# Experts' products on four 128x32 column parts, and routing steps placed by another estimate

## The chip, the cores and the metric

The kernel runs on one core of a Trainium2 chip. TensorE (PE) multiplies, VectorE (DVE), ScalarE (ACT) and GpSimd (POOL) compute, and SyncE (SP) issues most transfers. The metric is the device time of one launch in microseconds: the median of 3 runs is 492.07 (491.12 to 495.2).

## What is computed

```python
scores = scale * np.matmul(q, k.transpose(0, 1, 3, 2))      # batch 8, 12 heads, 448 tokens, 64 each
scores = cap * np.tanh(scores / cap)
attn = softmax(scores); x = (attn @ v) as 3584 tokens x 768
logits = x @ w_gate                                          # 8 experts
expert_idx = np.argmax(logits, axis=1); gate_w = its softmax weight
for e in range(E):
    tok_idx = tokens of expert e; if over 80, the 80 of largest gate_w are kept
    h = np.maximum(x[tok_idx] @ w1[e], 0.0)                  # 768 -> 1024
    out[tok_idx] = gate_w[tok_idx, None] * (h @ w2[e])       # 1024 -> 768, other rows zero
```

All is float32.

## The kernel before

Attention runs in 24 units: 8 batches, and in each three groups of four heads. A unit has seven tiles of scores (`scores`, L1152 and L1160) in two PSUM buffers, each followed by a tanh on ScalarE (L1161), then four exponentials (`expo`, L1165). GpSimd adds exponents for the divisor (`esum`, L1171). One unit later TensorE multiplies by the values (`av` L1192, `rests` L1223 and L1225), VectorE turns the divisor (`sums` L1233), scales (`scaled` L1245) and transposes (`turned` L1253). Units in DIRECT (20 and 23) take the divisor by products of ones instead (`total_of` L1210). The order in a unit is the string STEPS; unit 0 uses it too.

Behind every third unit a batch is routed: logits (L1270), their turn (`lt` L1285), the choice and key (L296 to L316), and the rank of every token's key among its expert's, by comparisons on VectorE that TensorE adds up (`ranks`, `late_ranks`: `psk`, `gb`, `pd`). Batches 0 to 4 are pruned first (`prt` L634, `prk` L649), so that experts 0 to 3 of the list can start early: their rows are gathered from DRAM by GpSimd (L783) and laid by VectorE (L678). Experts 4 and 5 have to wait for all batches (L756, L783, L1561). `background` places these steps between the steps of a unit: three lists (urgent, low, bg) of steps with a cost in ns, which it holds against clocks of TensorE and VectorE, by the tables PLACE and SLACK.

LAST is the order of the passage: the values of unit 23, and in between the six chunks of expert 0's first product (`begin`). Then come the products of six experts, 6 chunks of w1 (768x1024) and 8 of w2 (1024x768) each, as `chunk` writes them (L842): 96 token columns stationary, weights moving, F32. For expert 4 and 5's first product and expert 3 to 5's second, `wsplit` splits each weight chunk into two rounded halves on ScalarE (L830) and VectorE (L832), and three faster products take the place of one. SP loads the weights (L823) into 8 buffers that are filled during attention and 6 more. `turn` transposes the hidden rows (L870, L879), `put` scales by the gate (L899) and GpSimd stores the rows by an indirect transfer (L900).

## Time and profile before

| | us |
|---|---|
| median of 3 runs | 492.07 |
| profiled run | 495.86 |
| its span | 494.1 |
| TensorE busy | 459.2 (93%) |
| ScalarE busy | 338.6 (69%) |
| VectorE busy | 273.5 (55%) |
| GpSimd busy | 219.3 (44%) |
| TensorE's mean granted clock | 0.976 of 2.4 GHz |

The busy times are shares of the whole span; the stages of the program have different limits, so windows by stage are read beside them. Times in rows count from the start of the span.

### The profile page before, as it was taken

The numbers are of one execution on the slowest core, as the hardware profiler recorded it, in microseconds if no ns is written. First come the engines' busy times: TensorE is split into PE (matmuls) and PEld (weight loads), VectorE is DVE, ScalarE is ACT, GpSimd is POOL, SyncE is SP. The second block draws the span as 40 slices with busy tenths as digits, with TensorE's granted clock in tenths as the row PEclk, the third lists the DMA queues.
The fourth block names the chain that finished last, engine by engine and source line by source line (L and its number), as shares of the span: only waits on it lengthen the run. The fifth ranks groups of instructions, "written<-read, shape, count | busy, mean of one in ns | idle before, by whom it ended". The sixth has DMA issues, their size and how long they took to land. (4 is left out here: it accounts for less than half of the span.)

```text
span 494.1 us, 18314 instructions
## 1 busy us (share of the span) xinstructions
PE 459.2 (93%) x7945; PEld 232.1 (47%) x7945; DVE 273.5 (55%) x785; ACT 338.6 (69%) x360; POOL 219.3 (44%) x136
## 2 busy tenths in 40 slices
PE   7799999999999999999999989968999999975992
PEld 4244544544444544444454534532345445653781
DVE  1033374355456557645756928750658595657682
ACT  3999899899989889979888977950022101456681
POOL 0577656656656656666566315624150001440000
PEclk9999999999999999999999999997999999988897
DMA  6557687696596596676258576551099998999411
GB/s 161 146 170 197 192 238 222 185 257 190 168 257 192 158 290 192 190 194 167 87 126 218 141 213 168 162 190 36 8 342 391 400 359 263 334 398 356 123 62 27
DMA packets 67768, 100.89 MB, mean 204 GB/s; under 512 B 12208, under 2 KB 50128, under 8 KB 67680
## 3 DMA queue, kind: packets, MB, share of 16 engines
q1 hardware_dynamic: 66048, 96.23, 64.1%
q0 software_dynamic: 1440, 3.25, 2.0%
q8 instruction: 64, 1.05, 0.9%
q14 instruction: 24, 0.20, 0.1%
q10 hardware_dynamic: 192, 0.17, 0.1%
HBM read 76.11 MB, written 23.80 MB: 202 GB/s over the span
## 5 line engine op out<-in xcount | busy, mean ns | idle before, releaser
L1161 ACT ACTIVATE e<-sc 128x896 f32<-128x896 f32 x168 | 150.8, 913 | 35.7 <-PE sc L1160 24.7
L1192 PE MATMUL av<-e,vr 64*32 64x448 f32 x2304 | 161.1, 539 | 1.5 <-DVE x L1245 1.5
L1160 PE MATMUL sc<-qt,kt 64*32 64x448 f32 x2304 | 144.7, 545 | 4.9 <-ACT e L1161 3.4
L1165 ACT ACTIVATE e<-e 128x896 f32<-128x896 f32 (+1 forms) x96 | 144.7, 1507 | 0.8
L1171 POOL TENSOR_TENSOR t<-e 128x896 f32<-128x896 f32 x44 | 92.9, 2111 | 95.3 <-ACT e L1165 95.3
L1173 POOL TENSOR_TENSOR t<-t,e 128x896 f32<-128x896 f32 x44 | 92.9, 2112 | 36.5 <-ACT e L1165 34.8
L1192 PEld LDWEIGHTS av<-e,vr 64*32 64x32 f32 x2304 | 54.8, 107 | 58.1 <-issue 45.6
L1233 DVE STREAM_TRANSPOSE st<-sp 128x448 f32<-128x448 f32 x24 | 15.6, 650 | 118.4 <-PE sp L1192 96.5
L1160 PEld LDWEIGHTS sc<-qt,kt 64*32 64x32 f32 x2304 | 43.7, 107 | 52.0 <-issue 36.2
L842 PE MATMUL hp<-w,xt 128*96 128x512 f32 x96 | 45.5, 616 | 4.9 <-DVE xt L678 4.9
L1225 PE MATMUL av<-e,vr 64*32 64x224 f32 x384 | 44.3, 349 | 0.0
L1192 PE MATMUL sp<-t,ones 64*32 64x448 f32 x352 | 42.9, 536 | 0.0
L1225 PE MATMUL av<-e,vx 64*32 64x224 f32 x384 | 42.3, 350 | 0.0
L900 POOL DMA_INDIRECT out_dram<-ysv,si x6 | 6.1, 1016 | 81.0 <-ACT ysv L899 73.3
L1245 DVE TENSOR_TENSOR x<-av,r 128x448 f32<-128x448 f32 x48 | 27.7, 620 | 17.9 <-PE av L1192 17.8
L842 PE MATMUL yp<-w,thv 128*96 128x384 f32 x96 | 32.1, 487 | 0.0
L1225 PEld LDWEIGHTS av<-e,vr 64*32 64x32 f32 x384 | 22.0, 107 | 19.0 <-issue 18.6
L423 DVE TENSOR_SCALAR_CACHE_REDUCE gb<-krow,kc 112x896 bf16<-112x896 f32 (+7 forms) x36 | 30.1, 883 | 0.0
L1223 PE MATMUL sp<-e,ones 64*32 64x224 f32 x384 | 28.8, 350 | 0.0
L1253 DVE STREAM_TRANSPOSE xb<-x 128x448 f32<-128x448 f32 x48 | 27.9, 619 | 0.0
L1152 PE MATMUL sc<-qt,kt 64*32 64x224 f32 x768 | 25.6, 361 | 2.2 <-DMA qt<-in_q_dram 1.4
L842 PEld LDWEIGHTS hp<-w,xt 128*96 128x96 f32 x96 | 15.2, 167 | 26.2 <-issue 20.5
(281 smaller groups left out, 549.5 us busy)
## 6 DMA issues: line engine op xcount, KB each, us to landing
w<-in_w_dram SPq DMA_DIRECT2D x36, 512.0 KB
w<-in_w_dram SPq DMA_DIRECT2D x48, 384.0 KB
vr<-in_v_dram SPq DMA_DIRECT2D x24, 512.0 KB
out_dram<-zero SPq DMA_DIRECT2D x14, 768.0 KB
xs<-xb SPq DMA_DIRECT2D x32, 336.0 KB
kt<-in_k_dram SPq DMA_DIRECT2D x46, 224.0 KB
qt<-in_q_dram SPq DMA_DIRECT2D x46, 224.0 KB
vx<-in_v_dram SPq DMA_DIRECT2D x48, 32.0 KB
```

The lines of the kernel that those rows point to most:

```text
L423: nc.vector.tensor_scalar(g, krow[:, x:y], kp, 0.0, op0=ALU.is_ge, op1=ALU.add, accum_out=a)
L842: nc.tensor.matmul(ps[nn][:, 0:m] if isinstance(ps, tuple) else ps[:, nn, 0:m], a[:, kk, :], bb[:, nn * m:(nn + 1) * m], start=(kk == 0 an ...
L1160: nc.tensor.matmul(ps[32 * m:32 * m + 32, h, :S], st["k", u][w, pr, y:y + 32], st["q", u][w, pr], start=True, stop=True)
L1161: nc.scalar.activation(st["e", u][:, 2 * x:2 * x + 2], ps[:, :, :S], AF.Tanh, scale=st["regs"][0])
L1165: nc.scalar.activation(e, e, AF.Exp, scale=st["regs"][1])
L1171: nc.gpsimd.tensor_tensor(t1, e[:, 0:2], e[:, 2:4], op=ALU.add)
L1173: nc.gpsimd.tensor_tensor(st["es", u, pr], st["es", u, pr], e[:, 4:6], op=ALU.add)
L1192: behind(nc.tensor.matmul(ps[32 * g:32 * g + 32, :S], v_, e, start=first, stop=final))
L1223: behind(nc.tensor.matmul(st["sp", u][32 * g:32 * g + 32, HQ * i:HQ * i + HQ], ones[w, 0:32], e, start=(part == 0), stop=False))
L1225: behind(nc.tensor.matmul(st["av", u, f][32 * g:32 * g + 32, HQ * i:HQ * i + HQ], last_of(u, pr, h, i)[w, 32 * f:32 * f + 32], e, start=Fa ...
L1245: nc.vector.tensor_tensor(st["x", u][:, f], st["av", u, f][:, :S], st["r", u], op=ALU.mult)
L1253: nc.vector.transpose(st["xt", b][:, :, j, :], st["x", u][:, f].rearrange("p (a b) -> p a b", b=32))
```

## The change

Each chunk of an expert's weights is multiplied in four column parts: for a group of 32 tokens the same 128x32 stationary tile stands in four column strips, and each strip takes a quarter of the weight columns. The results lie on 128 partitions, so `relu`, `turn` and `put` work on 128 partitions, and a quarter row is stored per index: three indirect transfers of 128 quarter rows per expert instead of one of 96 rows. Gates are gathered three times for four experts together and copied. Nothing is split or rounded any more. Ten more weight buffers follow the first eight instead of six.

The scale of tanh and exp is a 128x1 pointer instead of a register. Unit 0 runs by FIRST, with the tile of the last keys (`q0`, `e3`) at its end. Unit 20 takes its divisor by `esum`. Two tiny VectorE steps get a summed output. `background` has a fourth list (fill), new costs, and steps that name what they need and what they finish.

```diff
-WMORE = 6
-AHEAD = 2
-DIRECT = (20, 23)
-WHOLE = (4, 3)
+WMORE = 10
+DIRECT = (23,)
...
-                nc.vector.tensor_scalar(usb, u, 2.0 ** -28, None, op0=ALU.max)
+                nc.vector.tensor_scalar(usb, u, 2.0 ** -28, 0.0, op0=ALU.max, op1=ALU.add, accum_out=dump[:C])
...
-                nc.gpsimd.indirect_dma_start(out=gt0[:, v:v + 1], out_offset=None, in_=gd[0:OB * S],
...
+    def gates_at(to, sg, g, n, m):
+        nc.gpsimd.indirect_dma_start(out=to[0:32 * n, g:g + 1], out_offset=None, in_=gd[0:m],
+                                     in_offset=bass.IndirectOffsetOnAxis(ap=sg[0:32 * n, g:g + 1], axis=0))
...
-    def wsplit(fp, w, n, tag):
-
-        hi = fp.tile([128, F], F32R, name=f"wh{tag}", tag="wh", bufs=AHEAD + 1)
-        nc.scalar.copy(hi[:, :n], w)
-        lo = fp.tile([128, F], F32R, name=f"wl{tag}", tag="wl", bufs=AHEAD + 1)
-        nc.vector.tensor_tensor(lo[:, :n], w, hi[:, :n].bitcast(F32), op=ALU.subtract)
-        return hi, lo
+    def rows_of(x, kk):
+
+        return lambda g: x[:, kk, 32 * g:32 * g + 32]
+
+    def turned_rows(x, kk):
+
+        j, b = divmod(kk, 2)
+        return lambda g: x[:, 2 * g + b, 32 * j:32 * j + 32]
+
+    def spot(ps, g, n):
+
+        return ps[g // 2][:, QF * (g % 2):QF * (g % 2) + n] if isinstance(ps, tuple) else ps[:, g // 2, QF * (g % 2):QF * (g % 2) + n]
 
     def chunk(ps, x, w, kk, last, n):
 
-        m = n // 2
-        pairs = [(x[0], w[0]), (x[1], w[0]), (x[0], w[1])] if len(w) == 2 else [(x[-1], w[0])]
-        terms = [(nn, i) for i in range(len(pairs)) for nn in range(2)]
-        for nn, i in sorted(terms) if kk == last else terms:
-            a, bb = pairs[i]
-            nc.tensor.matmul(ps[nn][:, 0:m] if isinstance(ps, tuple) else ps[:, nn, 0:m], a[:, kk, :], bb[:, nn * m:(nn + 1) * m],
-                             start=(kk == 0 and i == 0), stop=(kk == last and i == len(pairs) - 1))
+        q = n // 4
+        of = (rows_of if n == F else turned_rows)(x, kk)
+        for g in range(NG):
+            for j in range(4):
+                nc.tensor.matmul(spot(ps, g, q)[32 * j:32 * j + 32], of(g), w[:, q * j:q * j + q],
+                                 start=(kk == 0 and g % 2 == 0), stop=(kk == last and g > 0))
...
+        for i in range(2 * NG):
+            nc.tensor.transpose(hv[:, i], hs[:, i], cst("ident"))
+        nc.scalar.copy(th, hv)
+        return th
...
-            nc.scalar.activation(ys, yp[:, :, 0:DM // 2], AF.Copy, scale=gt)
...
+            for g in range(NG):
+                nc.scalar.activation(ys[:, g], spot(yp, g, QD), AF.Copy, scale=gt[:, g:g + 1])
+        for g in range(NG):
+            w = nc.gpsimd.indirect_dma_start(out=out.rearrange("t (i c) -> (t i) c", c=QD), out_offset=bass.IndirectOffsetOnAxis(ap=si[:, g:g + 1], axis=0),
+                                             in_=ys[:, g], in_offset=None, bounds_check=4 * T - 1, oob_is_err=False)
...
-            nc.scalar.activation(st["e", u][:, 2 * x:2 * x + 2], ps[:, :, :S], AF.Tanh, scale=st["regs"][0])
+            nc.scalar.activation(st["e", u][:, 2 * x:2 * x + 2], ps[:, :, :S], AF.Tanh, scale=scl)
...
-            nc.scalar.activation(e, e, AF.Exp, scale=st["regs"][1])
+            nc.scalar.activation(e, e, AF.Exp, scale=capt)
...
-            for q, last in ((urgent, 1), (low, 3), (bg, 2)):
+            for q, last in ((urgent, 1), (low, 3), (bg, 2), (fill, 4)):
...
-                        if now[0] < now[last] + gap or (n in (0, 1) and clock[0] < max(st["read"], ready_at[last] if gap else 0)):
+                        need = getattr(f, "needs", None)
+                        if need is not None:
+                            if clock[0] < max(st["read"], done.get(need, 1e18)):
+                                break
+                        elif now[0] < now[last] + gap or (n in (0, 1) and clock[0] < max(st["read"], ready_at[last] if gap else 0)):
                             break
...
-        st["regs"] = [nc.scalar.alloc_register(n) for n in ("sclr", "capr")]
-        for reg, t in zip(st["regs"], (scl, capt)):
-            nc.scalar.reg_load(reg, t[0:1, 0:1].bitcast(I32))
...
+        FIRST = "q1 q2 q3 e0 q4 p00 q5 e1 p01 l q6 e2 p10 p11 q0 e3".split()
...
-            todo = STEPS if w < NU else LAST
+            todo = FIRST if w == 0 else STEPS if w < NU else LAST
```

How the order moves, at three places.

TensorE's first tiles, unit 0 (`sc0_n`: tile n of unit 0; tile 0 holds the last keys of all four heads, tiles 1 to 3 belong to the first pair). Before, and now:

```order
L1152 MATMUL sc0_0_212<-qt0_156,kt0_157 32x224 x16
L1160 MATMUL sc0_1_230<-qt0_156,kt0_157 32x448 x8
L1160 MATMUL sc0_2_241<-qt0_156,kt0_157 32x448 x8
L1160 MATMUL sc0_3_251<-qt0_156,kt0_157 32x448 x8
...
L1160 MATMUL sc0_6_291<-qt0_156,kt0_157 32x448 x8
L1152 MATMUL sc1_0_312<-qt1_205,kt1_206 32x224 x16
```

```order
L1205 MATMUL sc0_1_211<-qt0_155,kt0_156 32x448 x8
L1205 MATMUL sc0_2_221<-qt0_155,kt0_156 32x448 x8
L1205 MATMUL sc0_3_231<-qt0_155,kt0_156 32x448 x8
L1205 MATMUL sc0_4_242<-qt0_155,kt0_156 32x448 x8
...
L1197 MATMUL sc0_0_285<-qt0_155,kt0_156 32x224 x16
L1197 MATMUL sc1_0_311<-qt1_204,kt1_205 32x224 x16
```

Tile 0 went from the first place to the last of its unit.

TensorE around the passage: the multiplication that gathers the places (`prt`, 20 products of which the first stands here), the key transposes (`prk`) and expert 0's first product (`hp0`). Before, and now:

```order
L1160 MATMUL sc23_4_5495<-qt23_5175,kt23_5176 32x448 x8
...
L634 MATMUL prt_5522<-prrh_5397,prlh_5172 96x40
...
L1160 MATMUL sc23_5_5543<-qt23_5175,kt23_5176 32x448 x8
...
L1160 MATMUL sc23_6_5595<-qt23_5175,kt23_5176 32x448 x8
...
L649 MATMUL prk0_5671<-ctt_74,prx_5586 112x96 x4
L649 MATMUL prk1_5677<-ctt_74,prx_5586 112x96 x4
L842 MATMUL hp0_5693<-w0_0_4869,xt0_0_109 96x512 x2
...
L842 MATMUL hp0_5693<-w0_1_4871,xt0_0_109 96x512 x2
```

```order
L1205 MATMUL sc22_4_5323<-qt22_4977,kt22_4978 32x448 x8
...
L652 MATMUL prt_5352<-prrh_5193,prlh_5032 96x40
...
L1205 MATMUL sc22_5_5380<-qt22_4977,kt22_4978 32x448 x8
...
L1205 MATMUL sc23_4_5589<-qt23_5198,kt23_5199 32x448 x8
...
L667 MATMUL prk0_5616<-ctt_74,prx_5462 112x96 x4
L1205 MATMUL sc23_5_5622<-qt23_5198,kt23_5199 32x448 x8
...
L667 MATMUL prk1_5663<-ctt_74,prx_5462 112x96 x4
L1205 MATMUL sc23_6_5669<-qt23_5198,kt23_5199 32x448 x8
...
L891 MATMUL hp0_5756<-w0_0_4911,xt0_0_110 32x256 x12
...
L891 MATMUL hp0_5756<-w0_1_4913,xt0_0_110 32x256 x12
```

`prt` moved from unit 23 to unit 22, `prk` from behind unit 23's scores to between them, and a chunk is twelve products of 32x256 instead of two of 96x512.

VectorE at the same stretch: the table of places (`prtk`, `tks`), the row numbers for the gathers (`gi0`), expert 0's rows (`xt0_0`), the sums of units 22 and 23 (`st22`, `st23`) and batch 5's gates (`w25`, `grow`). Before, and now:

```order
L1233 STREAM_TRANSPOSE st22_5562<-sp22_5448 128x448
...
L654 TENSOR_TENSOR prtk_5590<-tab_96 96x4
L656 COPY tks_104<-prtk_5590 32x4 x3
...
L662 TENSOR_SCALAR gi0_105<-prga_5627 32x12 x4
...
L678 STREAM_TRANSPOSE xt0_0_109<-xge0_0_5683 128x6x32
L678 STREAM_TRANSPOSE xt0_0_109<-xge0_1_5685 128x6x32
L678 STREAM_TRANSPOSE xt0_0_109<-xge0_2_5687 128x6x32
L1233 STREAM_TRANSPOSE st23_5752<-sp23_5662 128x448
```

```order
L672 TENSOR_TENSOR prtk_5466<-tab_96 96x4
L674 COPY tks_104<-prtk_5466 32x4 x3
...
L784 TENSOR_SCALAR gi0_105<-prga_5471 32x12 x4
...
L1278 STREAM_TRANSPOSE st22_5641<-sp22_5528 128x448
...
L691 STREAM_TRANSPOSE xt0_0_110<-xge0_0_5701 128x6x32
L691 STREAM_TRANSPOSE xt0_0_110<-xge0_1_5703 128x6x32
L691 STREAM_TRANSPOSE xt0_0_110<-xge0_2_5705 128x6x32
...
L330 SCALAR_TENSOR_TENSOR w25_5806<-tau5_5038,rd5_5042 112x32
...
L339 STREAM_TRANSPOSE grow_80<-gcol_79 128x32
L1278 STREAM_TRANSPOSE st23_5867<-sp23_5744 128x448
```

The row numbers moved ahead of the sums of unit 22, and batch 5's gates ahead of those of unit 23.

## Rows read from the trace of the kernel before

**Rows 1.** the head of the page.

```profile
span 494.1 us, 18314 instructions
```

**Rows 2.** windows of the run: length; busy us of PE, PEld, DVE, ACT, POOL; PEclk, DMA share, GB/s.

```profile
9.71:327.94 318.23, 309.92 (x7138) 146.94 (x7124) 171.77 (x485) 284.98 (x282) 185.81 (x88) 1.00 0.69 190
327.94:357.60 29.66, 24.23 (x205) 8.77 (x204) 11.71 (x51) 1.42 (x5) 8.79 (x10) 0.88 0.15 46
357.60:484.64 127.04, 118.58 (x558) 71.98 (x556) 88.65 (x243) 50.02 (x69) 22.79 (x26) 0.96 0.82 295
...
382.85:395.20 12.35, 12.35 (x41) 5.44 (x40) 7.16 (x15) 2.25 (x3) 1.28 (x2) 1.00 1.02 399
```

**Rows 3.** what TensorE waited for: us in total, times, longest us.

```profile
PE hp L842 <- DVE xt L678: 4.9, 1, 4.9
PE hp5a L842 <- ACT xh L1562: 4.5, 1, 4.5
PE sc L1160 <- ACT e L1161: 3.4, 4, 1.4
...
PE psk L404 <- DVE kc L316: 1.9, 1, 1.9
PE sc L1160 <- issue: 1.5, 1, 1.5
PE av L1192 <- DVE x L1245: 1.5, 1, 1.5
```

**Rows 4.** TensorE in the experts' stage: start us, us, engine, line, operation, count.

```profile
354.12 7.03 PE L842 MATMUL hp<-w,xt 128*96 128x512 f32 x16
360.98 0.83 PE L870 MATMUL htv<-ctt,hsv 96*128 96x96 f32 x8
361.74 1.96 PE L842 MATMUL hp<-w,xt 128*96 128x512 f32 x4
363.62 1.34 PE L1270 MATMUL lgp<-x,wgt 128*32 128x224 f32 x24
```

**Rows 5.** routing on TensorE in the experts' stage by line: busy us, mean ns.

```profile
L512 PE MATMUL pd<-ones_b,gb 112*128 112x1 bf16 x45 | 1.7, 164 | 0.3 <-DVE gl L487 0.2
...
L1270 PE MATMUL lgp<-x,wgt 128*32 128x224 f32 x24 | 1.3, 357 | 0.0
...
L1270 PEld LDWEIGHTS lgp<-x,wgt 128*32 128x32 f32 x24 | 0.7, 109 | 1.0 <-issue 0.8
```

**Rows 6.** the logits' weight loads, columns as in rows 4.

```profile
363.62 0.92 PEld L1270 LDWEIGHTS lgp<-x,wgt 128*32 128x32 f32 x24 [0.79 <-issue]
```

**Rows 7.** ScalarE by line and shape: busy us, mean ns, idle before.

```profile
L899 ACT ACTIVATE ysv<-yp,gt 96x768 f32<-96x768 f32 x4 | 3.6, 897 | 18.2 <-PE yp L842 14.0 <-DMA out_dram<-ysv,si 2.4 <-issue 1.8
...
L872 ACT COPY thv<-htv 128x768 f32<-128x768 f32 x3 | 2.4, 799 | 11.5 <-PE htv L870 11.5
```

**Rows 8.** the start: TensorE, columns as in rows 4.

```profile
5.17 1.13 PE L1152 MATMUL sc<-qt,kt 64*32 64x224 f32 x16 [0.74 <-DMA kt<-in_k_dram]
```

**Rows 9.** the first tanh on ScalarE, columns as in rows 4.

```profile
9.71 0.92 ACT L1161 ACTIVATE e<-sc 128x896 f32<-128x896 f32 x1 [5.93 <-PE sc L1152]
```

**Rows 10.** VectorE in batch 5's routing, columns as in rows 4.

```profile
233.45 1.87 DVE L315 TENSOR_SCALAR us<-u 112x4 f32<-112x4 f32 x1
```

**Rows 11.** VectorE as attention ends: sums, places, rows of expert 0.

```profile
323.66 0.65 DVE L1233 STREAM_TRANSPOSE st<-sp 128x448 f32<-128x448 f32 x1 [2.67 <-PE sp L1192]
...
335.54 0.38 DVE L678 STREAM_TRANSPOSE xt<-xge 128x192 f32<-128x192 f32 x1 [0.83 <-DMA xge<-xs,gi]
```

**Rows 12.** TensorE as attention ends.

```profile
335.97 3.73 PE L842 MATMUL hp<-w,xt 128*96 128x512 f32 x4 [4.87 <-DVE xt L678]
```

**Rows 13.** GpSimd: first gather of late rows, and the last store.

```profile
425.71 1.00 POOL L783 DMA_INDIRECT xgv<-xs,gi  x1 [7.03 <-DVE sz L774]
...
485.81 0.92 POOL L900 DMA_INDIRECT out_dram<-ysv,si  x1 [7.43 <-ACT ysv L897]
```

**Rows 14.** VectorE: last part of expert 4's rows laid.

```profile
434.65 0.38 DVE L1561 STREAM_TRANSPOSE xt<-xgv 128x192 f32<-128x192 f32 x1 [1.07 <-DMA xgv<-xs,gi]
```

More of the change, by code (lines that the diff above doesn't have):

```diff
@@ L56 @@
 LATER = OB * NQ + 1
-SLACK = (5500, 4000, 2500, 1500, 1800, 8000)
+SLACK = (6700, 5200, 3700, 1800, 2000, 9350)
 LATE = 3
@@ L391, in final_order, with known, waits @@
         return f0, f1, f2, f6, f3, f4, f5, f8
+    def known(f, done=None, needs=None):
+        if done is not None:
+            f.done = done
+        if needs is not None:
+            f.needs = needs
+        return f
+    def waits(f, n=1):
+        f.waits = n
+        return f
     def ranks(krow, gp, pl, b, acc, dfc, x0, c0, blocks, gw=GW):
@@ L535, in late_ranks @@
                 yield rest(i)
-        yield 200, use(1, after), 1
-        yield 200, use(-1, add), 1
+        yield 20, use(1, after, 600), 1
+        yield 130, use(-1, add), 1
     def fold(eng, t, dst):
@@ L690, in prune @@
+        yield 450, known(heads, "heads"), 0
+        yield 20, known(use(0, counts, 500), needs="heads"), 1
         steps = order(sm)
         for i, f in enumerate(steps):
[L692 to L694 removed]
+            yield 600 if f is steps[-1] else 750 if i == 1 else 450, waits(f), int(i == 0)
@@ L695, in prune @@
+        yield 2050, waits(lambda: z.update(r=ranked(sm, OCOL, acc, dfc, higher(sm, neso, cst("gt", C).rearrange("p (a e) -> p a e", a=E), "o"))), 2), 0
+        yield 500, places, 0
         for i in range(2):
-            yield 900, lambda i=i: parts(i), 0
-        for i in range((OCOL + 7) // 8):
-            yield 1500, lambda i=i: left(i), 0
+            yield 700, waits(lambda i=i: parts(i)), 0
+        for i in range((OCOL + 3) // 4):
+            yield 500, waits(lambda i=i: left(i)), 0
@@ L707, in prune @@
+        yield 700, waits(early), 0
+        yield 900, waits(rows_in), 0
+        yield 1900, waits(rows_out), 0
         for h in range(2):
-            yield 200, use(0, lambda h=h: rows(h)), 1
+            yield 20, use(0, lambda h=h: rows(h), 700), 1
         yield 50, lambda: low.extend(first_rows()), 0
@@ new lines, in gate_rows, with gates_of @@
+    def gate_rows(a, sg, n):
+        for e in range(n):
+            nc.vector.tensor_scalar(sg[32 * e:32 * e + 32], a[:, e], 0.25, -1.0, op0=ALU.mult, op1=ALU.add)
+    def gates_at(to, sg, g, n, m):
+        nc.gpsimd.indirect_dma_start(out=to[0:32 * n, g:g + 1], out_offset=None, in_=gd[0:m],
+                                     in_offset=bass.IndirectOffsetOnAxis(ap=sg[0:32 * n, g:g + 1], axis=0))
+    def gates_of(fp, packed, e, tag):
+        gt = fp.tile([128, NG], F32, name=f"gt{tag}", tag="gt")
+        for i in range(4):
+            nc.scalar.copy(gt[32 * i:32 * i + 32], packed[32 * e:32 * e + 32])
+        return gt
@@ new lines, in scatter_rows, with indices @@
+    def scatter_rows(tile_of, tk, a, si, sg=None):
+        o = tile_of("to")
+        nc.vector.tensor_scalar(o, tk, 0.0, BIG, op0=ALU.is_equal, op1=ALU.mult)
+        nc.vector.tensor_tensor(o, o, tk, op=ALU.add)
+        for i in range(4):
+            w = slice(32 * i, 32 * i + 32)
+            nc.vector.tensor_scalar(si[w], o, float(i - 4), None, op0=ALU.add)
+            if sg is not None:
+                nc.vector.tensor_scalar(sg[w], a, 0.25, -1.0, op0=ALU.mult, op1=ALU.add)
+    def indices(sm, tk, n, packed=None):
+        a = sm.tile([32, n, NG], F32, name="ga", tag="ga")
+        gi, si, sg = [sm.tile([128, n, NG], I32, name=x, tag=x) for x in ("gi", "si", "sg")]
+        gather_rows(a, tk, gi, T)
+        scatter_rows(lambda key: sm.tile([32, n, NG], F32, name=key, tag=key), tk, a, si, sg if packed is None else None)
+        if packed is not None:
+            gate_rows(a[:, packed], sg[:, 0], packed.stop - packed.start)
+        return gi, si, sg
@@ L1382, in background @@
                     n = getattr(f, "uses", None)
-                    if getattr(f, "two", False) and not st["late"]:
-                        cost += 600
-                    if st["late"]:
-                        cost = 20 if n in (0, 1) else {1700: 1950, 1500: 1100, 300: 20, 100: 20}.get(cost, 0.9 * cost)
+                    if not st["late"]:
+                        cost += 300 * getattr(f, "waits", 0)
                     if n in (0, 1) and len(st["held"]) == len(st["banks"]):
@@ L1409, in laid @@
             while v not in st["laid"]:
-                q, last = (low, 3) if low and (not bg or 0 not in st["laid"]) else (bg, 2)
+                q, last = (low, 3) if low and (not bg or 0 not in st["laid"] or v == "gates") else (bg, 2) if bg else (fill, 4)
                 run(q.pop(0)[1], last)
```

399 lines of the change are left out of this document (171 added, 228 removed).

## The prediction, made before the changed kernel ran

> **What bounds the kernel now.** I read the windows first, cut where the program changes stage. Attention, from the first tanh at 9.71 to the last exp at 327.94, takes 318.2 us with TensorE busy for 309.9 and ScalarE for 285.0 [rows 2]: TensorE bounds it, ScalarE has 33 us of room. The passage from attention to the experts (last values, expert 0's first product) takes 29.7 us with TensorE busy for only 24.2, at a mean granted clock of 0.88. The experts' stage then takes 127.0 us, 118.6 of them busy. Behind the last product lie 494.1 - 484.6 = 9.4 us [rows 1]. Second come TensorE's waits, which say where the other time goes: 4.9 us for the rows of expert 0, 4.5 for the split rows of expert 5, and 1.5 to 1.9 us at three places in attention [rows 3]. Third comes the timeline of the experts' stage: a 128-row chunk of the first product costs 6.86 us / 4 = 1.715 us (sixteen instructions of 512 columns, 354.12 to 360.98) [rows 4].
>
> The sum is made against the profiled run, 495.86 us, which is 3.8 above the median of 492.07; the prediction takes the 3.8 off again.
>
> **The experts' products (largest term).** A chunk's weights become the moving operand in four 128x32 parts that are to run side by side: 24 instructions of 256 columns (first product) or 192 (second), in six rounds of four. The nearest row is the logits, of exactly that shape with 224 columns: 24 matmuls in 1.34 us, each 0.357 long, so the sixth round begins at 0.98 and five rounds take 0.197 us each at most [rows 4, 5]. The floor is the column rate of the chunk itself, 1.715 us / 2048 = 0.84 ns, or 0.188 us for 224. I take the floor, because a chunk runs on where the logits start and end: 6 x 0.215 = 1.29 us, and 6 x 0.161 = 0.965 us. At the upper price they are 1.35 and 1.01. Thirty chunks of the first product and 48 of the second remain after expert 0's first: 38.7 + 46.3 = 85.0 us (88.9 at most). Six turns take as many columns as before, 360.98 to 361.74 or 0.76 us each: 4.6. Routing that shares TensorE: logits 1.3 and the counted comparisons 1.7 [rows 5], and an estimated 2.6 for the gathering of places and the small transposes: 5.6. Together 95.2 us.
>
> The splitting of weights on ScalarE and VectorE (L830, L832) goes with its rounded copies, and with it the wait for expert 5's split rows [rows 3]. What is late next is the weights. 84 chunks are 37.75 MB, eight are loaded early, and 33.55 MB at the 399 GB/s of a saturated stretch [rows 2] are 84.1 us. Tokens, stores and gathered rows in the same stretch are an estimated 4 MB, 10 us. The other ten buffers can be filled once the last values are done, some 4 us before expert 0's product ends, so loading ends about 90 us after it, and the last chunk is wanted at 94. That is nearly a tie, so I add 2 us for single waits: 97.2 against 127.0, a gain of **29.8**.
>
> Three small stores take the place of one at an expert's end. Five times this lies beside the next product. The last time it does not: GpSimd issued the one store in 0.92 us [rows 13], and two more behind it, an estimated 1.25 us each (the 0.92 and the pause that GpSimd makes between such issues), less a shorter scaling, cost **1.4** (0.5 to 2.5).
>
> **The passage.** The rows of expert 0 were laid at 335.92, and the place table that leads to them was read behind the sums of unit 22 at 323.66 [rows 11]. The product waited 4.87 us for them and then ran its first chunk in 3.73 us instead of 1.72 [rows 12]: twice the time, so at 1.2 GHz, the lower of its two levels, which the stage's mean of 0.88 bears out. Now the places are multiplied a unit earlier (second place of the order), the row numbers are written ahead of those sums, and the gathers have a unit in which to land. The 4.9 us go, half a microsecond of other idling (29.66 - 24.23 - 4.87), an estimated 2.3 of half clock, and 6 x (1.715 - 1.29) = 2.5 of faster chunks: **10.2**. The two key transposes and a logit turn that move into attention cost there what they save here, about 1.5 us.
>
> **Attention.** Gone should be the wait on `kc` (1.9): its cause is a floor of four elements a row that took 1.87 us [rows 10], and the new form writes a sum beside it, as the steps around it do. Gone too the wait on `x` (1.5), since the late place steps no longer lie ahead of it. Unit 20 no longer takes its divisor from 12 direct products: 1.5 us of idling at that change [rows 3] and an estimated 0.5 of products. GpSimd adds that unit's exponents again, as it does beside 22 other units. Together 4.9.
>
> Against this, 168 tanh and 96 exp now take their scale from a 128x1 pointer. The trace has no tanh with one. The scaling with a pointer takes 897 ns for 768 columns, a copy without takes 799 [rows 7]: 98 ns, or 25.9 us over 264 instructions. ScalarE's 285.0 become 310.9, beside TensorE's 309.9. Bounds: nothing, if the operand is fetched under the instruction before; and above, since the 25.9 are less than the 33 of room, half of them. In the first unit TensorE already waits 3.4 us for ScalarE [rows 3], and that grows by 11 x 0.098 = 1.1 at least; units without routing, in which TensorE is the shorter, add a few tenths each. I take 4 (0 to 12). Net in attention: a gain of **0.9**.
>
> **The start.** TensorE could start at 5.17 [rows 8], but the first tanh waited for a tile that needs both head pairs, until 9.71 [rows 9]. The keys that need both now come last, so the first tanh can follow one tile of 0.9 us and its latency: about 6.6, a gain of **3.1** (1 to 3.1).
>
> **Sum.** -29.8 + 1.4 - 10.2 - 0.9 - 3.1 = -42.6: 495.86 becomes 453.3, and on the scale of the median 449.5. I say **449.5**.
>
> **Rivals.**
>
> *Late rows or weights in the experts' stage.* Expert 4's rows are now gathered from 425.71 and laid by 435.03 [rows 13, 14], 77.4 us behind expert 0's product; then they will be wanted at about 3 x 15.5 + 7.7 + 3 x 0.76 + 5.6 = 62. VectorE's ranking must get 15 us shorter. If it comes late, or the weights fall a tenth below 399 GB/s, 3 to 6 us are lost, and part of it again to the lower clock, as in [rows 12]: 453 to 458. For it: the tie above. Against it: all splitting of weights (L832) leaves VectorE, which is busy 88.7 us in this stage [rows 2], and expert 0's rows leave the passage. Chance 0.18.
>
> *ScalarE bounds attention.* With 310.9 beside 309.9, two buffers of scores give little slack, and 6 to 12 us more appear: 455 to 461. For it: the equality. Against it: TensorE waited for ScalarE nowhere behind the first unit. Chance 0.14.
>
> *The new estimate does not bring the rows of expert 0 in time.* The wait returns with its half clock: 449.5 + 7 = 456. The order speaks against it. Chance 0.05.
>
> *Pointer free, no waits among the experts.* 449.5 - 4 - 2 = 443. Chance 0.09.
>
> *Slower: the parts' weight loads are not hidden.* All four parts use the same 128 rows. If each round had to wait for its loads, 0.109 us long each [rows 5], 78 chunks x 6 x 0.109 = 51 us come on top: 500. It ends above the old time as soon as a round costs 0.092 us more than counted (43 / 468). Against it: the 24 loads of the logits lie within 0.92 us while 24 matmuls of the same shape end within 1.34 [rows 4, 6]; loads in turn with six rounds of 0.36 would take over 2.6. Chance 0.03.
> The Trainium skill ("TensorE: Matmul & The Clock Gate", Part 3, The mechanism) says that a weight load overlaps matmuls in flight only when its row group differs, which is this rival's rule; by it the sum would be the 500 above, and the row of the logits disagrees with it.
>
> **How the numbers follow.** The forecast (445 to 453) has the remaining 0.51. The range from 440 to 460 holds it, the free pointer, the late rows and most of the ScalarE case; outside lie the tail of the latter and the slow case. About 1% (5 us) is what a measurement can tell from no change. Only the slow case ends within or above that: faster 0.95, same 0.02, slower 0.03.
>
> **What would show it.** In the new profile: first tanh near 6.6; first tanh to last exp near 317 with ScalarE busy near 311 (285 would mean a free pointer); no wait of TensorE for `xt0`; a first-product chunk every 1.29 us and a second every 0.965; from expert 0's product to the last one 97 us at 390 to 400 GB/s with the clock at 1.00; 10.8 behind it. I would be wrong if the four parts start one after another, if TensorE waits for `w` or for rows in more than single places, or if ScalarE runs without a gap through attention while TensorE waits for `e`.

## The result: 474.79 us, 4% faster, and 25 us above the forecast

The changed kernel takes 474.79 us (median of 4 runs, 472.17 to 475.75) where the kernel before, run beside it, takes 493.63. The ratio is 0.96, with a 95% interval from 0.9513 to 0.9686. The forecast was 449.5 in a range from 440 to 460. Four of its five stage terms came out within 4 us; attention was to take 317.3 us and took 334.3.

### The profile page after: what moved, and what is told of

It reads as the page before. It is cut to its first block, busy times and chain, and to the rows that moved or that the text cites. A ratio compares the mean times of both kernels' runs of the same rounds, so it can differ in the third digit from the quotient of the medians.

```text
span 472.3 us, 21423 instructions
## 1 busy us (share of the span) xinstructions
PE 437.2 (93%) x9533; PEld 224.0 (47%) x9533; DVE 244.4 (52%) x769; ACT 331.9 (70%) x349; POOL 239.7 (51%) x152
## 4 chain that ended last, share of the span: by engine, by line
PE 62%; ACT 14%; DVE 12%; DMA 6%; issue 4%; POOL 1%; SPq 0%; POOLq 0%; DVEq 0%
PE sc L1205 16%; PE av L1237 16%; PE hp L891 8%; ACT e L1206 8%; ACT e L1210 6%; DMA w<-in_w_dram 5%; PE yp L891 4%; PE sp L1237 3%; PE lgp L1316 2%; PE sp L1268 2%; DVE x L1290 2%; PE av L1270 2%; DVE w L319 2%; PE hp5a L891 1%; PE pd L447 1%
## 5 line engine op out<-in xcount | busy, mean ns | idle before, releaser
L1206 ACT ACTIVATE e<-sc,scl 128x896 f32<-128x896 f32 x168 | 164.1, 1002 | 21.2 <-PE sc L1205 21.1
L1210 ACT ACTIVATE e<-e,capt 128x1792 f32<-128x1792 f32 (+1 forms) x96 | 153.5, 1599 | 0.8
L1216 POOL TENSOR_TENSOR t<-e 128x896 f32<-128x896 f32 x46 | 96.9, 2107 | 90.6 <-ACT e L1210 90.1
L1218 POOL TENSOR_TENSOR t<-t,e 128x896 f32<-128x896 f32 x46 | 97.4, 2118 | 41.1 <-ACT e L1210 36.8
L1205 PEld LDWEIGHTS sc<-qt,kt 64*32 64x32 f32 x2304 | 39.8, 106 | 56.5 <-issue 34.6
L1278 DVE STREAM_TRANSPOSE st<-sp 128x448 f32<-128x448 f32 x24 | 15.6, 650 | 91.0 <-PE sp L1237 84.8
L941 POOL DMA_INDIRECT out_dram<-ysv,si x18 | 18.6, 1035 | 61.2 <-ACT ysv L939 53.5
L891 PE MATMUL hp<-w,xt 128*32 128x256 f32 x720 | 42.4, 381 | 2.3 <-DVE xt L691 1.4
L891 PE MATMUL yp<-w,thv 128*32 128x192 f32 x960 | 41.9, 327 | 0.6 <-DMA w<-in_w_dram 0.4
L1290 DVE TENSOR_TENSOR x<-av,r 128x448 f32<-128x448 f32 x48 | 27.7, 619 | 16.4 <-PE av L1237 16.3
L891 PEld LDWEIGHTS yp<-w,thv 128*32 128x32 f32 x960 | 30.1, 110 | 10.4 <-DMA w<-in_w_dram 2.4
L891 PEld LDWEIGHTS hp<-w,xt 128*32 128x32 f32 x720 | 21.9, 109 | 20.1 <-DMA w<-in_w_dram 3.4
```

The source lines that it names most:

```text
L891: nc.tensor.matmul(spot(ps, g, q)[32 * j:32 * j + 32], of(g), w[:, q * j:q * j + q], start=(kk == 0 and g % 2 == 0), stop=(kk == last and ...
L1205: nc.tensor.matmul(ps[32 * m:32 * m + 32, h, :S], st["k", u][w, pr, y:y + 32], st["q", u][w, pr], start=True, stop=True)
L1206: nc.scalar.activation(st["e", u][:, 2 * x:2 * x + 2], ps[:, :, :S], AF.Tanh, scale=scl)
L1210: nc.scalar.activation(e, e, AF.Exp, scale=capt)
L1216: nc.gpsimd.tensor_tensor(t1, e[:, 0:2], e[:, 2:4], op=ALU.add)
L1218: nc.gpsimd.tensor_tensor(st["es", u, pr], st["es", u, pr], e[:, 4:6], op=ALU.add)
```

## The profile after

The windows of the changed kernel, cut as in [rows 2]: attention, passage, experts, and what lies behind the last product (length; busy us of PE, PEld, DVE, ACT, POOL; clock, DMA share, GB/s).

```profile
6.22:340.53 334.31, 315.13 (x7176) 145.46 (x7167) 186.38 (x530) 307.97 (x285) 200.24 (x98) 0.99 0.67 187
340.53:359.50 18.97, 17.56 (x314) 7.95 (x302) 9.94 (x50) 0.76 (x2) 4.93 (x6) 1.00 0.29 83
359.50:460.63 101.13, 99.65 (x2033) 66.69 (x2025) 46.73 (x186) 20.76 (x57) 30.53 (x34) 1.00 0.96 357
460.63:472.30 11.67, 0.16 (x4) 0.00 (x0) 0.42 (x1) 0.68 (x2) 2.95 (x3) 0.74 0.12 30
```

Passage and experts fell from 29.7 and 127.0 us to 19.0 and 101.1, at a full clock. Attention grew by 16 us. TensorE is busy there for 315.1 of 334.3 us and idle for 19.2, where it was idle for 8.3 before, so most of the growth is waiting; ScalarE has 26 us left. What TensorE waited for (us in total, times, longest), to be read beside [rows 3]:

```profile
PE sc L1205 <- ACT e L1206: 8.3, 11, 2.9
PE av L1237 <- DVE x L1290: 6.8, 7, 1.3
PE prk L667 <- DVE lg L301: 1.8, 1, 1.8
PE sc L1197 <- ACT e L1206: 1.6, 1, 1.6
PE hp L891 <- DVE xt L691: 1.4, 1, 1.4
...
PE hp L891 <- DMA w<-in_w_dram: 0.8, 1, 0.8
```

The waits that were to go have gone: `kc`, and most of that for the rows of expert 0 (1.4 for 4.9). In their place the next unit's value products wait seven times for the scaled `x`. One of the seven, and a place of another kind at 237 us, on VectorE (start us, us, engine, line, operation, shapes):

```profile
65.47 0.65 DVE L1278 STREAM_TRANSPOSE st<-sp 128x448 f32<-128x448 f32 x1 [1.85 <-PE sp L1237]
...
67.28 0.14 DVE L317 TENSOR_SCALAR_CACHE_REDUCE rd<-tau 112x32 f32<-112x32 f32 x1
...
67.85 1.82 DVE L319 TENSOR_TENSOR w<-tau,rd 112x32 f32<-112x32 f32 x1
...
70.01 0.16 DVE L323 SCALAR_TENSOR_TENSOR kc<-u,wsc 112x4 f32<-112x4 f32 x1
70.08 1.15 DVE L1290 TENSOR_TENSOR x<-av,r 128x448 f32<-128x448 f32 x2
...
237.29 1.89 DVE L305 TENSOR_TENSOR d<-mx,lg 112x32 f32<-112x32 f32 x1
```

on GpSimd beside them,

```profile
67.52 2.11 POOL L1218 TENSOR_TENSOR t<-t,e 128x896 f32<-128x896 f32 x1 [1.85 <-ACT e L1210]
...
237.05 2.08 POOL L1216 TENSOR_TENSOR t<-e 128x896 f32<-128x896 f32 x1 [0.52 <-ACT e L1210]
```

and on TensorE behind them (the last two rows are of the experts):

```profile
70.76 1.14 PE L1237 MATMUL av<-e,vr 64*32 64x448 f32 x9 [1.28 <-DVE x L1290]
...
240.39 1.33 PE L1205 MATMUL sc<-qt,kt 64*32 64x448 f32 x16 [2.87 <-ACT e L1206]
...
355.60 6.68 PE L891 MATMUL hp<-w,xt 128*32 128x256 f32 x120
362.21 0.87 PE L919 MATMUL htv<-ctt,hsv 128*128 128x128 f32 x6
```

The key (L317 to L323) now stands between the sums (L1278) and the scaling (L1290). One of its steps, `w`, takes 1.82 us where others of its kind take 0.19, and it ends where GpSimd's addition ends (67.52 + 2.11 = 69.63). So does `d` at 237 us (239.13): ScalarE's `tau` waits 2.2 us for it, the next tanh stands behind `tau`, and TensorE waits 2.87.

Beside [rows 4], five chunks of expert 0's first product, 355.60 to the turn at 362.21, are 6.61 us or 1.32 each, for a forecast of 1.29. So the twenty-four loads of a chunk add almost nothing, and the four column parts do run side by side.

## The experiments

The first theory after the result was that the pointer scales cost the 17 us (theory P). Its rivals put it on VectorE's stretched steps (theory V): on their form (e2), or on where the new order puts the key (K: move it behind the scaling; O: move it ahead of the sums). Line numbers in rows are those of the kernel that the row is of. The table gives each one's stages from its profiled execution: the first tanh, the first 15 units (to the first tanh of unit 15), the last nine (to the end of the last exp), from there to the first turn, from the first turn to the last product, and the median of its runs.

| | first tanh | units 0-14 | units 15-23 | to turn | to last product | median |
|---|---|---|---|---|---|---|
| before | 9.7 | 194.1 | 124.2 | 33.0 | 123.7 | 493.63 |
| changed | 6.2 | 202.6 | 131.7 | 21.7 | 98.6 | 474.79 |
| e1_reg | 6.8 | 212.4 | 127.1 | 21.7 | 97.4 | 479.52 |
| e2_stt | 6.1 | 204.9 | 130.1 | 21.6 | 98.2 | 474.79 |
| e3_both | 6.1 | 213.7 | 130.5 | 21.7 | 98.4 | 482.86 |
| e4_ptr_before | 9.7 | 198.6 | 124.7 | 33.4 | 123.6 | 502.34 |
| e5_key_late | 6.9 | 205.3 | 131.5 | 21.5 | 98.5 | 478.31 |
| e6_key_late_reg | 7.1 | 203.2 | 128.4 | 21.7 | 98.2 | 472.76 |
| p0_parts | 9.8 | 193.4 | 122.0 | 28.6 | 122.3 | 489.90 |
| p0_first | 6.6 | 194.5 | 122.0 | 29.8 | 120.5 | 488.21 |
| e7_key_early * | 6.8 | 194.9 | 137.8 | 29.8 | 117.7 | 501.42 |
| e8_key_early_reg * | 6.9 | 191.9 | 135.1 | 25.8 | 120.3 | 495.31 |
| e9_single * | 6.2 | 192.5 | 139.6 | 32.1 | 118.4 | 502.85 |
| e10_direct * | 6.0 | 192.0 | 137.7 | 25.8 | 118.2 | 500.60 |
| e11_key_moved * | 6.8 | 195.7 | 131.4 | 29.1 | 115.1 | 494.34 |
| e12_key_moved_reg * | 6.1 | 192.0 | 134.1 | 30.6 | 116.8 | 491.76 |
| e13_moved_reg_d * | 6.3 | 201.4 | 133.1 | 30.8 | 115.3 | 502.58 |
| e14_moved_d * | 6.7 | 199.7 | 134.4 | 31.3 | 115.7 | 499.30 |
| e15_after_again | 6.1 | 204.2 | 130.3 | 21.5 | 100.1 | 474.84 |
| e16_moved_reg_again | 6.1 | 192.3 | 131.6 | 21.9 | 101.0 | 463.44 |

The runs with a star were made on another Trainium2 chip than e1 to p0_first, the last two on a third one; for the first two rows the record names no chip. The kernel before took 494.29, 495.17, 495.07, 495.39 and 495.46 us beside the five groups of runs, so it does not tell the chips apart; the stages behind attention do, as the last pair shows. Two programs stand there twice, each profiled once per row: the changed kernel (again as e15) and e12 (again as e16). Their stages of attention differ by up to 1.6 and 2.5 us, so smaller differences in the table say nothing.

### Registers, another form, and the pointer alone

e1 gives the changed kernel its registers back:

```diff
-AF.Tanh, scale=scl)
+AF.Tanh, scale=st["regs"][0])
...
-AF.Exp, scale=capt)
+AF.Exp, scale=st["regs"][1])
...
```

> The changed kernel with tanh and exp scaled from registers again, the rest as it is. Theory P (the pointer fills ScalarE's room: 264 x 0.09 = 23 us of work that was not there): attention falls from 334 us by 10 to 14, the run from about 474.5 to 460 to 465, TensorE's wait on e from 9.9 us to under 5. Theory V (VectorE's small steps, stretched to 1.8 us beside GpSimd and placed ahead of the scaling of the values and of ScalarE's tau, make TensorE wait): only 2 to 4 us, 470 to 472, the waits on x stay at 6.8 us.

e2 writes six steps with two operands as scalar_tensor_tensor, such as

```diff
-nc.vector.tensor_tensor(w, tau, rd, op=ALU.mult)
+nc.vector.scalar_tensor_tensor(w, tau, 1.0, rd, op0=ALU.mult, op1=ALU.mult)
...
```

> The changed kernel with pointers, but the six small two-operand steps of the key (d, oh, w) and of the pruned keys (prx, three) are written as three-operand steps, a kind that the trace never shows stretched. Same values. Theory V: none of them takes 1.8 us any more, the waits on x fall from 6.8 us to under 2, the wait on e at 237 us with its stretch of lower clock goes: 6 to 9 us, 465 to 468. Theory P: 0 to 3 us, 472 to 474, because ScalarE stays at 308 us of work.

e3 does both. e4 puts the pointers into the kernel before (e1's diff turned round).

> Both edits: registers and three-operand steps. If P and V are separate causes their gains add: 453 to 458. If one hides the other, it is no better than the better of the two.

> The kernel before with the pointers alone. Theory P: ScalarE's work in attention rises from 285 to 308 us and the run by 8 to 14 us (501 to 507). Theory V: by 1 to 4 us (494 to 497); the earlier first tanh (no register load) can give 0 to 2 back in both.

Theory P fell as the cause of the 17 us, and the cure by form too. Without the pointer (e1) ScalarE is 21 us less busy (286.5 for 308.0), and the kernel is 5 us slower: ratio to before 0.97 (0.9646 to 0.9755). The intervals of the two ratios overlap, but e3 against e2, which differ by the registers alone, shows the same clear of noise. The waits for `x` doubled:

```profile
PE av L1237 <- DVE x L1290: 14.0, 7, 3.0
```

ScalarE hands the exponentials over earlier, GpSimd's additions come earlier, and then they meet two steps of the key, where in the changed kernel they met one:

```profile
68.47 1.65 DVE L319 TENSOR_TENSOR w<-tau,rd 112x32 f32<-112x32 f32 x1
...
70.45 2.06 DVE L323 SCALAR_TENSOR_TENSOR kc<-u,wsc 112x4 f32<-112x4 f32 x1
```

Behind these waits the clock fell as well: over the first 15 units its mean is 0.97 of full, where the changed kernel has 1.00, and TensorE is 5.3 us busier there.

In e2 nothing moved (ratio 0.9605, 0.9557 to 0.9654; `x` 7.0). The new form still reads two operands from memory, and `w` was held in it as before. The forecast called it a form that the trace never shows stretched; the changed kernel's own trace already had a stretched one, at L330 (least, middle and longest ns). In e2, and then in the changed kernel:

```profile
L319 DVE SCALAR_TENSOR_TENSOR w<-tau,rd x8: 192/1007/1835, 70.0 to 374.2; 112x32 f32<-112x32 f32 x8
```

```profile
L330 DVE SCALAR_TENSOR_TENSOR w<-tau,rd x8: 176/186/1110, 74.8 to 398.2; 112x32 f32<-112x32 f32 x8
```

e3 (0.9755, 0.9702 to 0.9808) is as slow as e1: the two edits give no gain together either. In the kernel before, the pointer costs 8 us (ratio 1.0174, 1.011 to 1.0239), of which attention has 5.1. That is what theory P said of e4 (501 to 507), so the pointer has its price in the old order, but it doesn't explain the new one.

### The key behind the scaling, and the parts alone

e5 holds steps marked as waiting in the turn between sums and scaling, so that the key comes behind `x`; e6 adds the registers.

```diff
+                    if st.get("hold") and getattr(f, "waits", 0):
+                        break
...
+                    st["hold"] = w < NU and todo[:i].count('b') == 4
```

> The changed kernel, but in the turn between a unit's sums and its scaling no step that the planner marks as waiting on itself is placed, so the key of units 3 to 15 (L317 to L323) stands behind the scaling x, no longer ahead of it. Theory K (the new order puts the key ahead of x, VectorE's steps of two operands in memory stand still while GpSimd adds the exponentials beside them, x comes late and TensorE waits 0.4 to 1.3 us in each of seven units): TensorE's waits for x fall from 6.8 us to under 2 and the run to 466 to 470. Theory P (the pointer scales alone cost the attention its 17 us): TensorE waits for ScalarE instead, 473 to 476.

> The same, with the scales of tanh and exp read from two registers as in the kernel before, which takes 23 us off ScalarE's busy time. Theory K (registers were slower in the first test only because the additions of the exponentials then met the key more often): with the key out of the way they gain what they gained in the kernel before (8 us), 456 to 462. If the additions meet other steps in this order too: 466 to 476, with waits for x left over 4 us.

p0_parts is the kernel before (its planner, registers, costs, unit 0) with the new products, stores and gates; p0_first adds the new unit 0.

```diff
-            todo = STEPS if w < NU else LAST
+            todo = FIRST if w == 0 else STEPS if w < NU else LAST
...
```

> The kernel before with the experts' products on column parts alone: its planner, registers, two direct units, first unit and costs are the old ones. If the experts' stage is worth what the trace showed (passage 29.7 to 19.0, experts 127.0 to 101.1, tail 9.5 to 11.7) and the attention's 17 us come from the planner and the pointer: attention 318 to 321 us long, the run 459 to 463, below the changed kernel. If the column parts themselves cost the attention its time (their gates and places): 472 to 478.

> The same parts alone, with the first unit's last keys at its end as in the change. If the new first unit gives what its first tanh shows (6.2 for 9.7 us): 3 to 3.5 us below the parts alone, so 456 to 460. If the first unit's later end gives it back: within 1 us of the parts alone.

Behind the scaling the key is too late. The waits for `x` fell to 3.0 us in e5, but now the transposes of the keys wait, and TensorE waits longer for ScalarE (13.0 us for 8.3):

```profile
PE sc L1205 <- ACT e L1206: 13.0, 15, 2.9
PE psk L422 <- DVE kc L323: 5.2, 3, 1.7
PE av L1237 <- DVE x L1290: 3.0, 3, 1.6
```

e5 is 0.9652 of before (0.9598 to 0.9705), e6 0.9546 (0.9488 to 0.9604). Here the registers gain 5 us. Theory K in this form, key behind `x`, gave no gain by itself, and both runs missed its figures (466 to 470 and 456 to 462).

The parts alone tell two things apart. Their attention takes 315.4 us, so the new products are innocent of the 17 us. But the run is 490 (0.9879, 0.9806 to 0.9953): behind attention the old order loses what the products gain, with rows and weights late.

```profile
PE hp L878 <- DVE xt L1571: 8.2, 2, 7.6
PE pcp L763 <- POOL rh L748: 3.7, 1, 3.7
...
PE yp L878 <- DMA w<-in_w_dram: 3.3, 3, 1.8
PE hp L878 <- DVE xt L678: 2.6, 2, 2.4
PE hp L878 <- DMA w<-in_w_dram: 2.4, 2, 2.2
```

So both my figures for p0_parts missed, and those for p0_first with them, since I had added the stages up as if the order were free to be swapped. From the last exp to the end the changed kernel takes 131.8 us and p0_parts 163.3: the new order is worth some 30 us there, and with the pointer it costs 19 in attention. The new unit 0 gave 1.7 us by the medians (0.9844, 0.9779 to 0.991, intervals overlap); its first tanh came 3.2 us earlier.

### The key ahead of the sums, through the planner

e7 makes choice and key of batches 0 to 4 one step of the planner, e8 adds the registers:

```diff
-            urgent.append((1600, waits(lambda: st["math", b][1]()), 0))
-            urgent.append((1350, known(waits(lambda: st["math", b][2]()), ("key", b)), 1 if b < OB else "ordered"))
+            if b < OB:
+                urgent.append((2950, known(waits(lambda: (st["math", b][1](), st["math", b][2]())), ("key", b)), 0))
...
```

> The changed kernel (pointer scales), with choice and key of units 3 to 15 as one step, so that the key stands ahead of the next unit's sums, as in the kernel before. Theory O (the first 15 units lose 8.5 us, 202.6 for 194.1, all of it idle TensorE, because the new order puts the key between sums and scaling, and 4.5 us are the pointer's): the first 15 units take 198 to 200, as in the kernel before with the pointer (198.6), and the run 469 to 472. If VectorE's stretched steps cost the same wherever the key stands: no change, 474 to 476.

> The same with registers for the two scales. Theory O: the first 15 units take 194 to 196, as in the kernel before and in the parts alone (194.1 and 194.5), and the run 460 to 465, 8 to 12 under the key behind the scaling with registers. If registers collide here too: 468 to 475.

e9 also takes `d` in four steps with one operand and a pointer, and the three parts of the expert rows' keys by one reduction; e10 gives unit 20 its direct products back (`DIRECT = (20, 23)`).

```diff
-            nc.vector.tensor_tensor(d, up(mx), lg, op=ALU.subtract)
+            for c in range(NC):
+                nc.vector.tensor_scalar(d[:, c], lg[:, c], mx[:, c:c + 1], -1.0, op0=ALU.subtract, op1=ALU.mult)
...
```

> The same, and two kinds of VectorE's steps with two operands in memory are written with one: the distance d as four tensor_scalar steps, the three parts of the keys of expert rows summed by one reduction. Theory two operands (only steps that read two operands from memory stand still beside GpSimd's addition): d beside an addition takes under 0.3 us a piece where it took 1.89, ScalarE's tau is not late, unit 16 falls from 16.4 to under 14.5, and the run is 2 to 4 us below the one before it. If VectorE stands still whatever it reads: the pieces are stretched too, and the run is within 1 us.

> The same, with unit 20's exponentials summed by TensorE again, as in the kernel before, so that GpSimd has 14 us less to add in the last nine units. If GpSimd's additions are what holds those units (128.4 to 131.7 us for 122.0 in the parts alone): 1 to 3 us below the last one. If TensorE's own work counts: 1 to 2 us above it.

Theory O held in its stage: the first 15 units fell to 194.9 with pointers and 191.9 with registers. The runs as a whole did not: e7 and e8 lie some 30 us above their forecasts, and the four ratios are 1.0101, 1.0, 1.0142 and 1.0083. The time went at two places. The last nine units grew by 3 to 8 us; the joint step has a larger cost in the planner, which moves what is placed later, and that this is the reason was not tested. And the stages behind attention were 24 to 30 us longer, for the most part the chip's doing (below). In e9 the plain step with one operand was held too (least, middle and longest ns of 32 pieces), and the run came out 7.5 us above e8 where 2 to 4 below were hoped for:

```profile
L306 DVE TENSOR_SCALAR d<-lg,mx x32: 218/226/2133, 61.3 to 378.3; 112x8 f32<-112x8 f32 x32
```

e10 came 2.3 us below e9 by the medians, as its forecast had it, but the intervals of the two ratios overlap (1.008 to 1.0204, and 1.004 to 1.0126). Its last nine units still took 137.7 us.

### The key alone moved, and `d` in the summed form

e11 moves nothing but the key's instructions. The planner's clock sees no change, and TensorE's and ScalarE's orders are those of the changed kernel. e12 adds the registers.

```diff
-            urgent.append((1600, waits(lambda: st["math", b][1]()), 0))
+            urgent.append((1600, waits(lambda: (st["math", b][1](), st["math", b][2]() if b < OB else None)), 0))
...
-            urgent.append((1350, known(waits(lambda: st["math", b][2]()), ("key", b)), 1 if b < OB else "ordered"))
+            urgent.append((1350, known(waits(lambda: None if b < OB else st["math", b][2]()), ("key", b)), 1 if b < OB else "ordered"))
```

> The changed kernel with one thing moved: the key's instructions of batches 0 to 4 stand right behind the choice, ahead of the next unit's sums, and not between sums and scaling. The planner's clock and all orders of the other engines stay. Theory O (the key's place): the first 15 units fall from 202.6 us to about 194.5, as they did when the planner placed it there, the last nine units stay at 131.7 and the stage behind at 131.8, the run 465 to 468. Theory P (the pointer): the waits for x turn into waits for ScalarE, 472 to 475.

> The same with registers for the two scales. If registers were slower in the first test only because of the key's place: the first 15 units take 192, the last nine 128 to 130, the run 458 to 464, below the changed kernel by over 10 us. If registers lose here too: 467 or more.

e13 and e14 (registers and pointers) write `d` in the form that also gives its sum; the sign goes into the tanh.

```diff
+                nc.vector.tensor_scalar(d[:, c], lg[:, c], mx[:, c:c + 1], 0.0, op0=ALU.subtract, op1=ALU.add, accum_out=dump[:C])
...
-                nc.scalar.activation(tau, d, AF.Tanh, scale=0.5)
+                nc.scalar.activation(tau, d, AF.Tanh, scale=-0.5)
```

> The same, and d is made by four steps that read one operand and also write out their sum (the form of the step rd, which was never stretched), the three parts of the expert rows' keys are summed by one reduction. Theory second port (steps with two operands in memory, and plain ones of one operand in their fast form, stand still beside GpSimd's addition; the form that writes its sum doesn't): d's four pieces take under 0.3 us each beside an addition, ScalarE's tau of unit 16 is on time, unit 16 falls from about 16.4 to under 14.5 and the run by 2 to 4 us. If every step is stretched: no gain, or up to 4 us more as in the plain form.

> The same as the last, but with pointer scales. Against it, it prices the pointer where the waits of VectorE are gone: 23 us more ScalarE busy, of which units without routing show 0.5 each; 4 to 10 us slower. If ScalarE has room everywhere: within 2 us.

The key's place alone is worth 6.9 us in the first 15 units (202.6 to 195.7), and the waits for `x` fell from 6.8 to 1.4 us. With it out of the way the registers gain 3.8 more there (192.0), which is below the kernel before. The last nine units did not shrink. The runs as a whole, 0.9973 (0.9941 to 1.0005) and 0.9865 (0.9775 to 0.9955) of before, were 26 us and more above both forecasts. All but some 5 us of that lies behind attention, which raised the question of the chip.

`d` settles what holds VectorE. In the summed form no piece is held, though an addition runs beside four of them from 235.94 to 238.02 (the other 28 met none; in e14 it is four pieces again). The steps behind it with two operands from memory are held:

```profile
L306 DVE TENSOR_SCALAR_CACHE_REDUCE d<-lg,mx x32: 220/221/223, 60.6 to 380.8; 112x8 f32<-112x8 f32 x32
```

```profile
235.94 2.08 POOL L1216 TENSOR_TENSOR t<-e 128x896 f32<-128x896 f32 x1 [0.35 <-ACT e L1210]
238.10 2.10 POOL L1218 TENSOR_TENSOR t<-t,e 128x896 f32<-128x896 f32 x1
```

```profile
236.54 0.22 DVE L306 TENSOR_SCALAR_CACHE_REDUCE d<-lg,mx 112x8 f32<-112x8 f32 x1
...
237.60 0.47 DVE L309 SCALAR_TENSOR_TENSOR cand<-d,ctt 112x32 f32<-112x32 f32 x1
238.10 0.19 DVE L310 TENSOR_REDUCE cms<-cand 112x4 f32<-112x32 f32 x1
238.32 1.93 DVE L311 TENSOR_TENSOR oh<-ctt,cms 112x32 f32<-112x32 f32 x1
```

The gain did not come. Unit 16 took 15.8 us for 16.3, not under 14.5: four pieces take 1.0 us where one step took 0.19, so `tau` was late all the same. And the first 15 units grew from 192.0 to 201.4, with waits for `x` at 10.0 us, since the longer choice pushed the key back into the additions. e14, with pointers, was to be 4 to 10 us slower than e13 and wasn't: its first 15 units took 199.7 us. The four runs of e13 spread from 494.95 to 505.87 us, so its total says little.

### The same program on two chips

> The changed kernel, unaltered, on the chip of the next run. Theory chip (on the chip of e7 to e14 TensorE gets its instructions late in the experts' stage, whatever the order ahead of it): 490 to 500 us there, with some 20 us more between the first turn and the last product and waits for nothing named, if it is that chip; 472 to 477 if it is the first one. Theory order (the key's earlier place itself shifts the experts' stage into that state): 472 to 477 on either chip.

> The key moved and the scales in registers (as e12), beside the changed kernel on the same chip. Its attention is 326 us long for 334. Theory chip: 6 to 13 us below the changed kernel on the same chip, whichever chip it is (459 to 466 on the first, 485 to 492 on the other). Theory order: 488 to 495 on either chip, 15 to 20 above the changed kernel.

e15 is the changed kernel unaltered and e16 is e12 unaltered. On the third chip e15 took 474.84 us (0.9576 of before, 0.9546 to 0.9607) and e16 463.44 (0.932, 0.9283 to 0.9357). Theory chip held: the key's place does not bring on the longer stages behind attention. TensorE in five chunks of expert 0, the same program, e12 first:

```profile
347.88 4.50 PE L891 MATMUL hp<-w,xt 128*32 128x256 f32 x75
352.58 0.42 PE L891 MATMUL hp<-w,xt 128*32 128x256 f32 x2 [0.19 <-issue]
354.00 0.43 PE L891 MATMUL hp<-w,xt 128*32 128x256 f32 x2 [1.00 <-issue]
355.45 0.38 PE L891 MATMUL hp<-w,xt 128*32 128x256 f32 x1 [1.01 <-issue]
...
362.79 0.90 PE L919 MATMUL htv<-ctt,hsv 128*128 128x128 f32 x4
```

and e16:

```profile
345.30 6.68 PE L891 MATMUL hp<-w,xt 128*32 128x256 f32 x120
351.91 0.87 PE L919 MATMUL htv<-ctt,hsv 128*128 128x128 f32 x6
```

Within a chunk, some of whose products have already run, TensorE stops for a microsecond at a time and waits for nothing that the profile shows. From the last exp to the last product e12 takes 147.4 us and e16 122.9. Of these 24.5 us, 8.5 are idle time of TensorE (13.6 for 5.1); for the other 16 it is busy longer, at a mean clock of 0.90 and 0.94 of full in the two stages, where e16 has 1.00. What it is about the chip stays open. Attention differs by 2.1 us only, so the stages of attention in the starred runs can be read; their totals can't be compared with the others.

e16 beats both kernels: 11.4 us below the changed one beside it and 32.0 below the one before, by the medians.

## Why the prediction was wrong

The sum was made on the scale of the profiled run, 453.3, and that run took 474.13. The 20.8 us lie here: attention +17.0, experts +3.9, behind them +0.8, passage -0.5, start -0.4. The other 4.5 of the 25.3 are the scale: I took off 3.8 for the profiled run of before, and that of after lies 0.7 below its median.

**Attention is the step that failed**, and in it the gains. The forecast said "Gone too the wait on `x` (1.5), since the late place steps no longer lie ahead of it", and summed attention to a net gain of 0.9. That wait, at the passage, did fall to 0.8 us. But I had followed the order at the start, at the passage and at batch 5, not at batches 0 to 4, where the key went between sums and scaling. There it cost 6.9 us (e11), and five of the seven waits for `x` lie in the first 15 units, where the kernel before has none. [Rows 10] even showed a stretched step of 1.87 us. I read that as the cost of the step's form, and not as a step held by GpSimd, which any order could run into. It ended at 235.32, where GpSimd's addition ended in the kernel before (235.29):

```profile
233.22 2.07 POOL L1173 TENSOR_TENSOR t<-t,e 128x896 f32<-128x896 f32 x1
```

The new form does cure that step, `us`: it takes 0.16 us, also in the five places of e5 and e13 where an addition runs beside it. But `w`, `d` and `kc` kept a form that is held.

By the Trainium skill ("SBUF — State Buffer", Who interferes with whom) VectorE and GpSimd share a pair of SBUF ports, held by one of them at a time; a VectorE step with two inputs in SBUF contends with a GpSimd instruction that reads SBUF, a plain tensor_scalar can do so in a two-port mode, and its form that also writes out the accumulator does not. These traces agree: 1.82 and 1.89 us for 0.19, 2133 ns for 218, 222 at most in the summed form beside an addition; which mode a step ran in they do not show. I had not held that page against [rows 10].

**The pointer** was priced right by size: 4 (0 to 12); e4 shows 5.1 in attention and 8 in all, e11 against e12 3.8 in the first 15 units. Units without routing show it bare: from first tanh to first tanh, units 1 and 2 of e4 take 12.4 us and those of the kernel before 11.9. ScalarE's busy time came to 308.0 for 310.9. What I had not seen is that its sign depends on the order: where the key stands in the additions' way, slower exponentials helped by 5 us (e1). The rival "ScalarE bounds attention" had the symptom, waits for `e` of 9.9 us, but 2.87 of them came by way of `d` and VectorE.

**The last nine units** were not forecast to grow and did by 7.5 us: the sum had no term for it. TensorE waits 2.7 us more there and is busy 4.8 us more (124.2 for 119.4). The mean clock of the stage is 0.97 of full, where the kernel before has 1.00. It fell to the lower of its two levels at two places, right behind the wait of 2.87 us for `d`'s tanh and behind the one of 1.8 us for the key transposes of the expert rows (`prk`). The windows there (columns as in [rows 2]):

```profile
240.40:246.00 5.60, 5.60 (x88) 2.18 (x96) 2.44 (x11) 3.98 (x5) 0.94 (x1) 0.70 0.00 0
331.60:338.00 6.40, 6.39 (x96) 2.77 (x104) 1.78 (x5) 3.95 (x5) 4.26 (x5) 0.73 0.91 300
```

At mean clocks of 0.70 and 0.73, shares of 0.30 and 0.27 of these 5.60 and 6.40 us are lost, an estimated 3.4 us together. The rest of the busy time, some 1.4 us, fits the work that moved in, such as the key transposes. By unit, 16 is 3.5 us longer (the held `d`), 22 and 23 are 6.8 longer and 21 is 4.7 shorter. The growth came with the new order in every run that has it (127 to 140 us) and in none without (122.0 to 124.7). Which of its steps pay for the shorter stages behind was not settled; e9, e10 and e13 found no cure.

**Experts.** The mechanism was right, the size a little off. A first-product chunk took 1.32 us for 1.29. Seven second ones in a row (410.57, 7.16) took up to 1.02 for 0.965. Over 30 and 48 chunks that is up to 3.5 us of the 3.9, inside the bound of 88.9 that I gave; the remainder is not located. Single waits for weights add 1.2, for the 2 I allowed, at a DMA share of 0.96: the tie was real. The rival with loads that are not hidden is refuted by 1.32 us a chunk, and with it, for this case, the rule of the Trainium skill that it rests on ("TensorE: Matmul & The Clock Gate", Part 3, The mechanism).

**Passage, start, end** came as summed: 18.97 for 19.5, at a clock of 1.00 for 0.88; first tanh at 6.22 for 6.6; 11.67 for 10.8, where the three last stores took 2.95 us on GpSimd.

## What to carry to other kernels

When a change moves steps by a planner, follow one whole period of the order on the engine that feeds the bottleneck; I had read its ends. A small step whose duration jumps between 0.19 and 1.9 us was here a step held by a neighbour: look for the instruction that ends with it. Moving such steps paid (e11, e16), and writing them in another form did not in e2 and e13. And compare the totals of two kernels only from the same chip, stage by stage where the chips differ.
